# A fused attention and two mixture-of-experts layers: one block more in split products, later weight splits and unread products in gaps

## The chip, the cores and the metric

One core of a Trainium2 chip runs the whole program. The metric is device time in microseconds (us), the median of several executions. TensorE (PE) multiplies, VectorE (DVE), ScalarE (ACT) and GpSimd (POOL) do the rest, SyncE (SP) issues most DMAs. Each engine takes its instructions in the order of its own program and waits on semaphores for the others. A window's clock of 1.00 is TensorE at 2.4 GHz, 0.50 is 1.2 GHz.

## The reference

```python
def _attn_ref(q, k, v):                      # (4, 8, 576, 64)
    q_s = softmax of q over the last axis
    k_s = softmax of k over the sequence
    kv = np.einsum('bhsd,bhse->bhde', k_s, v)
    return np.einsum('bhsd,bhde->bhse', q_s, kv)

def _moe_ref(x, w_gate, w1, w2, capacity):   # x (2304, 512), 8 experts, F = 1024, capacity 576
    logits = x @ w_gate; expert_idx = np.argmax(logits, axis=1)
    # the first 576 tokens of each expert, in order, go through it
    h = np.maximum(np.einsum('ecd,edf->ecf', disp, w1), 0.0)
    y = np.einsum('ecf,efd->ecd', h, w2)
    out[i] = gate_w[i] * y[expert_idx[i], pos[i]]     # 0 for the others

def _moe2_ref(x, w_gate, w1, w2):
    logits = x @ w_gate; order = np.argsort(-logits.flatten())
    for idx in order:                        # greedy: the highest logit first
        tok, e = idx // E, idx % E
        if assigned[tok] >= 0 or counts[e] >= N // E: continue   # 288 tokens each
        assigned[tok] = e; counts[e] += 1
    for e in range(E):
        mask = assigned == e
        out[mask] = np.maximum(x[mask] @ w1[e], 0.0) @ w2[e]
```

## The kernel before

**Attention** comes first; its result goes to memory (`xd`) in rows of tokens, and the first layer's gate logits are formed on the way.

**First layer (`moe1`).** `route1` finds each token's expert and its place, `ilist` makes the list of rows of an expert, `X(t)` transposes 128 gathered rows and splits them into `xh` and `xl`. Products are made in three passes of a split format, hi x hi, lo x hi and hi x lo, each one pass of TensorE (`hidden`, L383 to L385, and L463 to L465). With the data of this run three experts have tokens: `body(0)`, `body(1)` and `last(2)`. `last` also forms the second layer's logits from that expert's rows: `diag` puts the gate weights on diagonals of a free part of `hl` (ACT copies the high parts, L487 subtracts for the low), `turn(g)` transposes a 64-column part of w2 on DVE, copies it on ACT into `w2h` and subtracts on DVE into `w2l` (L491), and `mul(g)` multiplies both parts with the diagonals into `pm`.

**Second layer (`moe2`).** Its tokens are assigned by a search in eight phases, one for each expert. A phase closes an expert and finds its cut among the sorted logits in six steps; a step is a comparison on DVE (`G`), eighteen small products on TensorE (`pc`), a decision on DVE (`sat`, `an`, `ii`), and the next step needs it. `ilist` of a phase then makes the row list (`pp`, `pk`, `pl`, `pz` are its products), and `gather` fetches 3 x 96 rows by indirect DMA into `xg`. This runs between the products of the expert blocks: a planner (`Search`, with model times `Q.pe` and `Q.dv`) adds up what each instruction should take, and puts a search step into the program where its inputs should be there. The order on each engine is thus fixed when the kernel is built.

A block `m` is one expert's 288 tokens: `first(m)` has eight column groups `f` (w1, relu, into `hT` or `hs`), `second(m)` four (`d`: w2, into `yT`). `X(m,d)` transposes the gathered rows, inside `second(m-1)`; `O(m,h)` transposes the results, inside `first(m+1)`, and scatters them. Blocks below `LATE` use plain fp32 products (a pair of TensorE instructions each). Blocks from `LATE` on use the split format: `sp1` and `sp2` make hi (ACT cast) and lo (DVE subtraction) of w1 and w2, into `w1hs`, `w1ls`, `w2hs`, `w2ls`, and the inputs are split as `xhs`, `xls` and `hhs`, `hls`. `sp1(m,k)` stands in `second(m-1)`, `sp2(m,k)` in `first(m)` at even `f`. Before block 0's rows are there, the planner spends `IDLE` us on search steps.

There are two buffers for w1 (`stage`, `w1b`), and one for w2 (`w2b`). `loads` issues a block's w1 when the block two before has no more use for its buffer (`f1`), and w2 when the block before has none (`f2`): at the end of `second(m-1)` for an fp32 block, and after the fourth `sp2` for a split one. `T`, `V` in this layer are wrapped (L770 is the wrapper's line, L777 after the change), so nearly all of the search and the blocks has that one line in the profile, and tiles tell them apart. After `first(4)` the few rows of the last three blocks go through `short` (L1107, L1116, L1128), which this run takes.

Of the kernel before, what the change touches and what calls it, by code (L numbers as in the profile page):

```python
# [324 lines left out]
def moe1(nc,tc,c0,tp,K,W,Q,xd,w1,w2,wg2,yd,L):  # L325

    V=nc.vector; G=nc.gpsimd; T=nc.tensor; A=nc.scalar
    with ExitStack() as ctx:
# [138 lines left out]
        def last(i):  # L467
# [13 lines left out]
            def diag():  # L481

                for r in range(4): A.copy(hl[:,4+r,256:512].rearrange("p (x y) -> p x y",x=2),bc(z1,1,2))
                for a in range(4):
                    p=slice(32*a,32*a+32)
                    d=hl[p,4:8,256:512].rearrange("p r (b a e) -> p r b a e",b=4,a=4)[:,:,:,a]; w=wq[p].rearrange("p (r b) e -> p r b e",r=4)
                    A.copy(d[:,:,:,0:8],w); G.tensor_tensor(d[:,:,:,8:16],w,d[:,:,:,0:8].bitcast(F32),op=ALU.subtract)  # L487
            def turn(g):
                w=wts[g%2]; V.transpose(w,S.w2[:,:,64*g:64*g+64])
                w=w.rearrange("p k (b j) -> p k b j",b=2)  # L490
# [17 lines left out]
            for hf,s in enumerate(ls_):  # L508
                for f in range(8):
                    if hf==0 and f in RS: next(rs,None)  # L510
                    if hf==0:
                        if f>3: mul(f-4)
                    else:
                        if f%2==0: sp2(f//2)
                        if f<4: mul(4+f)
                        if f==3: wlog(); V.tensor_tensor(oj,bc(K.ioj,1,5),bc(liL[:,:,1],2,NJ),op=ALU.is_equal)
                        if f==5:
                            pl=acc.tile([16,256],F32,name="plT",tag="acc"); lmul(pl,0,range(8)); A.copy(lT[0],pl)
                            pl=pst.tile([16,320],F32,name="plT",tag="t")
                        if f==6: lmul(pl,1,range(0,5))  # L520
                        if f==7: lmul(pl,1,(5,))
                    if hf or i: hidden(f,s)
                    if hf==0:
                        if f==1: diag()
                        turn(f)
            def logits():

                V.tensor_tensor(op,bc(K.iop,1,5),bc(liL[:,:,0],2,128),op=ALU.is_equal)
# [31 lines left out]
        def steps(i):  # L560
            if i+1==E:
                with tc.manual_schedule(): last(i)
                return
            with tc.If(n>i+1) as cmp:
                with tc.manual_schedule(): body(i)
                steps(i+1)
            with cmp.Else():
                with tc.manual_schedule(): last(i)
        with tc.manual_schedule():
            nc.sync.dma_start(wgs,wg2.rearrange("(c p) e -> p c e",p=128))  # L570
            for a in range(4): nc.sync.dma_start(wq[32*a:32*a+32],wg2.rearrange("(b i) e -> i b e",i=32))
            route=route1(nc,c0,psl,K,L); nxt=ilist(0)
            next(route)
            next(nxt); next(nxt)
            next(nxt)
            for _ in nxt: pass
            for k in range(4): sp1(k)
            for t in range(2): X(t,True)
            ld(2,0,A)
            for f in range(8):  # L580
                if f in R1: next(route,None)
# [192 lines left out]
class Search:  # L774


    def __init__(self,nc,tc,c,t,K,W,yd,w1,w2):  # L777
        self.nc=nc; self.c=c; self.t=t; self.K=K; self.W=W; self.yd=yd; self.w1=w1; self.w2=w2

        self.w1b=[W.stage.w1,None]; self.w2b=[None,None]  # L780
        self.gens=[]; self.ch=None; self.stop=None; self.blk=-1; self.psum=None; self.xgp=None
        self.pe=self.dv=0.0; self.vo=None
        self.V=Paced(nc.vector,self,self.vcost); self.T=Paced(nc.tensor,self,self.tcost)
        S=self.S=NS()
# [58 lines left out]
    def step(self,x):  # L843
        if x is self.ch and self.stop is not None and self.R[0].sl is not None:
            if self.stop==0:
                self.pe=max(self.pe,x[1]); x[1]=self.pe+0.2; return
            self.stop-=1
        self.pe=max(self.pe,x[1])
        try: r=next(x[0])
        except StopIteration: self.gens.remove(x); return  # L850
        x[1]=self.dv+LATV if r is None else self.dv-0.3 if r=="v" else self.dv+r[0] if type(r) is tuple else self.pe+r
# [4 lines left out]
        self.loads()  # L856
    def idle(self,x):

        for _ in range(int(x*10)): self.pe+=0.1; self.tick()
    def until(self,cond):  # L860

        while not cond():
# [106 lines left out]
    def loads(self):  # L969
# [3 lines left out]
        for b in range(E):  # L973
# [4 lines left out]
            if not B.l1 and (b<2 or self.B[b-2].f1) and (b<BUB or B.xg is not None):  # L978
                B.l1=True
                for k in range(2): nc.sync.dma_start(self.w1b[b%2][:,2*k:2*k+2],self.w1[bass.ds(B.e,1),256*k:256*k+256].rearrange("a (k p) f -> p (a k) f",p=128))  # L980
            if B.l1 and not B.l2 and self.w2b[0] is not None and (b<1 or self.B[b-1].f2):
                B.l2=True
                for k in range(2): nc.sync.dma_start(self.w2b[b%2][:,4*k:4*k+4],self.w2[bass.ds(B.e,1),512*k:512*k+512].rearrange("a (k p) f -> p (a k) f",p=128))


BUB=5
FEW=160
LATE=3


def moe2(nc,tc,t,K,W,Q,yd,w1,w2,out):
    V=Q.V; G=nc.gpsimd; T=Q.T
    with ExitStack() as ctx:
# [50 lines left out]
        def first(m):  # L1044
            r=R[m]; Q.blk=m
            for f in range(8):
                if m>=LATE and f%2==0: sp2(m,f//2)
                if m>0 and f in (1,2,3): O(m-1,f-1)

                if m==E-2 and f>3 and f<7: put(E-1,f-4,zr,False)  # L1050
# [87 lines left out]
        with tc.manual_schedule():  # L1138
            Q.psum=lambda shape,name: psr.tile(shape,F32,name=name,tag="rc")
            Q.xgp=b2  # L1140
            Q.until(lambda: R[0].xg is not None)
            Q.idle(IDLE)
            x0=[pool.tile([128,288],F32,name="pt2",tag=tag) for pool,tag in ((pst,"t"),(pst,"t"),(acc,"acc"),(acc,"acc"))]
# [2 lines left out]
            for u in range(3):  # L1146
                for d in range(4): T.transpose(x0[d][:,96*u:96*u+96],r.xg[:,u,128*d:128*d+128],K.ident[:96,:96])
            for d in range(4): nc.scalar.copy(r.x[:,d],x0[d])
            G.memset(zr,0.0)
            for m in range(BUB-1): first(m); second(m)  # L1150
            first(BUB-1)

# [17 lines left out]
DBG=False  # L1170


LATT=0.64; LATL=1.1; STOP=12; LATD=0.0; LATV=0.0; LATP=0.13; MARG=0.0; TXG=7.87; IDLE=6.63
RS=(1,3,5,7); R1=(1,3,4,6); X1=(2,3,4)


# [53 lines left out]
```

## Time and profile before

| | us |
|---|---|
| median of 3 executions | 613.84 (611.88 to 617.84) |
| profiled execution | 614.9 |
| its span in the trace | 613.2 |
| TensorE busy | 536.0 (87% of the span) |
| DVE busy | 349.6 (57%) |
| ACT, POOL busy | 170.3 (28%), 113.4 (18%) |
| mean granted clock | 0.94 |

The span is what the trace covers; the execution's own time holds 1.7 us more. Busy shares are means over stages with different limits. `x` behind a row is its number of instructions, `<-` in brackets says how long the engine was idle just before and who released it.

### The profile page before, as it was taken

Reading aid. Unit: us, or ns where it says so; the run is one execution under the profiler, and the core shown is the slowest. Engines: PE = TensorE matmul, PEld = TensorE weight load, DVE = VectorE, ACT = ScalarE, POOL = GpSimd, SP = SyncE. Lnnn points to the kernel's source line nnn. Section 1 sums busy time; section 2 is a strip of 40 time slices with the busy share of each in tenths; the row PEclk is TensorE's granted clock in tenths of the full one; section 3 lists DMA queues with packets and bytes.
Section 4 is the critical chain, followed back from the end, with each engine's and each line's share of the span. In section 5 each row is a group of like instructions: output and inputs, shape, how many; then the busy total and the mean of one; then the engine's idle time right before and its main releaser. Section 6 shows DMA issues by size and latency. Waiting matters only on the chain.

```text
span 613.2 us, 10394 instructions
## 1 busy us (share of the span) xinstructions
PE 536.0 (87%) x3995; PEld 450.3 (73%) x3995; DVE 349.6 (57%) x1103; ACT 170.3 (28%) x309; POOL 113.4 (18%) x126
## 2 busy tenths in 40 slices
PE   0699992799999999899995899999999849999993
PEld 0588882689889987898773666667666649999992
DVE  8789879494327331564675657475677747440000
ACT  2244422243323341443000111112023215442120
POOL 4051702203110311200112021030210012250011
PEclk9999997699999999799998698989999969999997
DMA  9982743796304250000044614433243085661401
GB/s 269 310 244 66 246 154 94 231 347 210 139 27 138 78 173 35 14 1 1 18 156 143 217 40 150 149 94 138 59 158 124 14 258 181 228 183 68 166 27 29
DMA packets 54004, 82.43 MB, mean 134 GB/s; under 512 B 11904, under 2 KB 33408, under 8 KB 53936
## 3 DMA queue, kind: packets, MB, share of 16 engines
q1 hardware_dynamic: 38416, 58.82, 29.6%
q0 software_dynamic: 5088, 15.93, 8.5%
q10 hardware_dynamic: 10432, 6.82, 3.7%
q8 instruction: 37, 0.61, 0.4%
q14 instruction: 31, 0.25, 0.1%
HBM read 63.86 MB, written 17.70 MB: 133 GB/s over the span
## 4 chain that ended last, share of the span: by engine, by line
PE 51%; DVE 10%; issue 9%; DMA 3%; ACT 2%; POOL 1%; another core or an unknown queue 0%; POOLq 0%; SPq 0%; ACTq 0%; DVEq 0%
PE pa L770 19%; PE pa L463 3%; PE pa L465 3%; PE pa L464 3%; PE pa L1128 3%; PE pa L1116 3%; PE pa L383 2%; PE pa L384 2%; PE pa L385 2%; PE pa L1107 2%; PE pc L770 2%; DVE G L770 1%; DMA xg<-yd,ib 1%; PE pg L431 1%; DMA w2b<-in_moe_w_dram 1%
## 5 line engine op out<-in xcount | busy, mean ns | idle before, releaser
L383 PE MATMUL pa<-xh,w1h 128*128 128x256 f32 (+1 forms) x192 | 60.1, 313 | 1.0 <-ACT xh L381 0.7
L384 PE MATMUL pa<-xl,w1h 128*128 128x256 f32 (+1 forms) x192 | 58.9, 307 | 0.1
L385 PE MATMUL pa<-xh,w1l 128*128 128x256 f32 (+1 forms) x192 | 58.7, 306 | 0.0
L770 PE MATMUL pa<-h,w2b 128*128 128x288 f32 x192 | 58.1, 433 | 0.0
L968 POOL DMA_INDIRECT xg<-yd,ib x21 | 21.3, 1012 | 122.8 <-issue 53.3
L770 PEld LDWEIGHTS <-G 128*31 128x31 bf16 (+2 forms) x756 | 23.9, 101 | 23.8 <-DVE G L770 13.1
L770 PE MATMUL pa<-x,stage 128*128 128x288 f32 x128 | 40.8, 451 | 0.1
L383 PEld LDWEIGHTS pa<-xh,w1h 128*128 128x128 f32 x192 | 38.3, 199 | 2.7 <-ACT xh L381 1.1
L770 PEld LDWEIGHTS pa<-h,w2b 128*128 128x128 f32 x192 | 34.2, 195 | 7.7 <-issue 0.9
L384 PEld LDWEIGHTS pa<-xl,w1h 128*128 128x128 f32 x192 | 38.3, 199 | 0.5 <-DVE xl L381 0.4
L385 PEld LDWEIGHTS pa<-xh,w1l 128*128 128x128 f32 x192 | 38.4, 200 | 0.0
L1025 POOL DMA_INDIRECT out_dram<-yn,ib x19 | 19.1, 1003 | 103.9 <-ACT yn L1033 52.0
L391 DVE SCALAR_TENSOR_TENSOR hl<-pa,hh 128x256 fp32r<-128x256 f32 (+1 forms) x48 | 21.5, 452 | 29.2 <-ACT hh L390 29.1
L402 POOL DMA_INDIRECT yd<-y,idx x15 | 15.0, 1001 | 112.9 <-ACT y L398 93.4
L770 DVE TENSOR_TENSOR G<-b,th 128x372 bf16<-128x372 f32 (+2 forms) x70 | 33.0, 509 | 1.2
L390 ACT ACTIVATE hh<-pa 128x256 fp32r<-128x256 f32 (+1 forms) x48 | 19.7, 410 | 49.2 <-PE pa L385 46.1
L463 PE MATMUL pa<-w2h,hh 128*128 128x512 f32 (+1 forms) x80 | 33.0, 413 | 0.0
L770 PE MATMUL pc<-g,G 128*31 128x8 bf16 (+2 forms) x756 | 27.8, 170 | 5.3 <-DVE G L770 4.5
L465 PE MATMUL pa<-w2h,hl 128*128 128x512 f32 (+1 forms) x80 | 31.5, 394 | 0.0
L464 PE MATMUL pa<-w2l,hh 128*128 128x512 f32 (+1 forms) x80 | 31.3, 391 | 0.0
L770 PEld LDWEIGHTS pa<-x,stage 128*128 128x128 f32 x128 | 23.6, 203 | 5.7 <-issue 0.4
L1053 ACT ACTIVATE h<-pa 128x288 f32<-128x288 f32 x24 | 9.8, 410 | 62.1 <-PE pa L770 62.1
(380 smaller groups left out, 1259.3 us busy)
## 6 DMA issues: line engine op xcount, KB each, us to landing
stage<-in_moe_w_dram SPq DMA_DIRECT2D x18, 1024.0 KB, 5.4
w2b<-in_moe_w_dram SPq DMA_DIRECT2D x12, 1024.0 KB, 5.9
w1b<-in_moe_w_dram SPq DMA_DIRECT2D x8, 1024.0 KB, 7.2
yd<-z ACTq DMA_DIRECT2D x1, 4608.0 KB, 26.5
km<-in_k_dram SPq DMA_DIRECT2D x4, 1024.0 KB, 10.1
vm<-in_v_dram SPq DMA_DIRECT2D x4, 1024.0 KB, 9.5
xd<-xs SPq DMA_DIRECT2D x8, 512.0 KB, 2.6
qm<-in_q_dram SPq DMA_DIRECT2D x3, 1024.0 KB, 10.4
```

The source lines that it names most:

```text
L383: T.matmul(ps,wh,xh_,start=first,stop=False)
L384: T.matmul(ps,wh,xl_,start=False,stop=False)
L385: T.matmul(ps,wl,xh_,start=False,stop=last)
L390: A.activation(hh[:,f,s],pa,AF.Relu)
L391: V.scalar_tensor_tensor(hl[:,f,s],pa,0.0,hh[:,f,s].bitcast(F32),op0=ALU.max,op1=ALU.subtract)
L463: T.matmul(pa,hh[:,k,ts],W.w2h[:,k],start=(k==0),stop=False)
L464: T.matmul(pa,hh[:,k,ts],W.w2l[:,k],start=False,stop=False)
L465: T.matmul(pa,hl[:,k,ts],W.w2h[:,k],start=False,stop=(k==7))
L770: return f(*a,**k)
L968: nc.gpsimd.indirect_dma_start(out=B.xg[:,h],out_offset=None,in_=self.yd,in_offset=bass.IndirectOffsetOnAxis(ap=B.idx[:,h:h+1],axis=0),bou ...
L1025: s_=G.indirect_dma_start(out=out,out_offset=bass.IndirectOffsetOnAxis(ap=R[m].idx[:,h:h+1],axis=0),in_=src,in_offset=None,bounds_check=N- ...
L1116: for k in range(4): T.matmul(pa,w1_[:,k,128*f:128*f+128],x[:,k,0:FEW],start=k==0,stop=k==3)
```

## The change

- `LATE` is 2: blocks 0 and 1 stay in fp32, blocks 2, 3 and 4 use split products (before: 3 and 4).
- The first split block (`m==LATE`) has its four `sp2` at `f` 4 to 7; later ones at even `f`, as before.
- Block 0's w2 load is issued behind its row copies: a flag `x0`, and a one-element ACT copy from the rows into `w2b` that the load has to wait for. `IDLE` falls from 6.63 to 2.2, so block 0's transposes come earlier in TensorE's program.
- `keep(n)` adds n products of a constant with itself, 128 x 128 in bf16, into a tile `pw` that nobody reads: 24, 36, 72, 10 and 6 in the first layer's opening, and some dozens in the wait for the second layer's first rows.
- In the last expert, the low parts in `diag` are subtracted on DVE instead of GpSimd, and the eight `turn`s are spread otherwise over the column groups: none at `f` 0, one at 1, two at 2, then one each.

```diff
@@ last(i): diag, and the column groups
-                    A.copy(d[:,:,:,0:8],w); G.tensor_tensor(d[:,:,:,8:16],w,d[:,:,:,0:8].bitcast(F32),op=ALU.subtract)
+                    A.copy(d[:,:,:,0:8],w); V.tensor_tensor(d[:,:,:,8:16],w,d[:,:,:,0:8].bitcast(F32),op=ALU.subtract)
...
-                        turn(f)
+                        for g in ((),(0,),(1,2),(3,),(4,),(5,),(6,),(7,))[f]: turn(g)
@@ moe1, opening
+        def keep(n):
+
+            pw=acc.tile([128,128],F32,name="pw",tag="acc")
+            for _ in range(n): T.matmul(pw,K.ones,K.ones,start=True,stop=True)
...
+            keep(24)
             next(route)
+            keep(36)
...
             for _ in nxt: pass
+            keep(72)
             for k in range(4): sp1(k)
-            for t in range(2): X(t,True)
+            X(0,True); keep(10); X(1,True); keep(6)
@@ Search
+        if self.keep and x[1]-self.pe>0.2: self.keep(int((x[1]-self.pe-0.1)*14))
         self.pe=max(self.pe,x[1])
...
-        for _ in range(int(x*10)): self.pe+=0.1; self.tick()
+        for z in range(int(x*10)):
+            if self.keep: self.keep(1+z%2)
+            self.pe+=0.1; self.tick()
...
-            if B.l1 and not B.l2 and self.w2b[0] is not None and (b<1 or self.B[b-1].f2):
+            if B.l1 and not B.l2 and self.w2b[0] is not None and (self.x0 if b<1 else self.B[b-1].f2):
...
-LATE=3
+LATE=2
@@ first(m)
-                if m>=LATE and f%2==0: sp2(m,f//2)
+
+                if m==LATE and f>3: sp2(m,f-4)
+                elif m>LATE and f%2==0: sp2(m,f//2)
@@ moe2, opening
+            pw=[]
+            def keep(n):
+
+                if not pw: pw.append(acc.tile([128,128],F32,name="pw",tag="acc"))
+                for _ in range(n): nc.tensor.matmul(pw[0],K.ones,K.ones,start=True,stop=True)
+            Q.keep=keep
             Q.until(lambda: R[0].xg is not None)
             Q.idle(IDLE)
...
             for d in range(4): nc.scalar.copy(r.x[:,d],x0[d])
+
+            nc.scalar.copy(Q.w2b[0][0:1,0,0:1],r.x[0:1,3,0:1]); Q.x0=True; Q.loads()
             G.memset(zr,0.0)
+            Q.keep=None
...
-IDLE=6.63
+IDLE=2.2
```

DVE before, at the start of block 3's first half, the first split block. `zh` ends an earlier row list, `w2ls` is the first subtraction of block 3's w2, and `scr` to `sb` belong to the search's last row lists; TensorE's `pp` reads `sb`.

```order
L770 TENSOR_TENSOR zh<-z_14162,z_13903 96x1
L770 TENSOR_TENSOR w2ls<-w2b,w2hs 128x1024
L770 SCALAR_TENSOR_TENSOR scr<-closed,r_69 128x8
L770 TENSOR_REDUCE e_966<-scr 128x1
L770 TENSOR_SCALAR ei_976<-e_966 1x1
L770 COPY w__947<-alive 128x18
L770 MEMSET w__947 128x18
L770 SCALAR_TENSOR_TENSOR sb<-rst_128,w__947 128x36
```

DVE after, in block 2's first half, now the first split block, from its third column group to the fifth (`hls` is the low part of one group's result, `G`, `sat`, `ii`, `th` are a search step).

```order
L777 SCALAR_TENSOR_TENSOR hls<-pa,hhs 128x288
L777 TENSOR_TENSOR G<-b,th 128x6x31
L777 TENSOR_TENSOR pre<-pre,ii 128x1
L777 TENSOR_SCALAR sat,an<-pc 31x8
L777 TENSOR_SCALAR ii<-pa_13922 128x1
L777 SCALAR_TENSOR_TENSOR th<-cand_122,ii,pre 128x31
L777 TENSOR_TENSOR G<-b,th 128x12x31
L777 SCALAR_TENSOR_TENSOR hls<-pa,hhs 128x288
L777 TENSOR_TENSOR w2ls<-w2b,w2hs 128x1024
L777 TENSOR_TENSOR G<-b,th 128x6x31
```

The subtraction of w2 has moved from ahead of everything in that half to behind the fourth `hls`, and the search's steps of phase 5 and 6 stand around it.

SP before, its loads from the fifth expert's number (`ei`) on: w2 is block 2's and the two DMAs of `stage` are block 4's w1.

```order
L977 TENSOR_LOAD ei_973
L977 ISA x2
L983 ISA
L983 DMA w2b<-in_moe_w_dram 128x4x512
L983 ISA
L983 DMA w2b<-in_moe_w_dram 128x4x512
L980 ISA
L980 DMA stage<-in_moe_w_dram 128x2x1024
```

SP after, from the same row.

```order
L987 TENSOR_LOAD ei_973
L987 ISA x2
L990 ISA
L990 DMA stage<-in_moe_w_dram 128x2x1024
L990 ISA
L990 DMA stage<-in_moe_w_dram 128x2x1024
L993 ISA
L993 DMA w2b<-in_moe_w_dram 128x4x512
```

Block 4's w1 now stands ahead of block 2's w2; the w2 loads of blocks 3 and 4 follow.

TensorE before, at the second layer's opening: the end of phase 1's last step (`pc`, 32 wide, and its count `pa`), and block 0's row transposes.

```order
L770 LDWEIGHTS G
L770 MATMUL pc<-g,G 32x8
L770 LDWEIGHTS onesb
L770 MATMUL pa_12421<-satb,onesb 128x8
L770 MATMUL pt_12447<-ident,xg_12272 128x96
L770 MATMUL pt_12448<-ident,xg_12272 128x96
```

TensorE after, in the same place.

```order
L777 LDWEIGHTS onesb
L777 MATMUL pa_12519<-an,onesb 128x1
L1157 LDWEIGHTS onesb
L1157 MATMUL pw<-onesb 128x128
L1157 LDWEIGHTS onesb
L1157 MATMUL pw<-onesb 128x128
...
L777 MATMUL pt_12530<-ident,xg_12425 128x96
L777 MATMUL pt_12531<-ident,xg_12425 128x96
```

The transposes stand three search steps earlier, and unread products fill the place ahead of them. In the blocks that follow, the halves (first, second, first, ...) of blocks 0 to 4 hold 6, 5, 6, 5, 6, 2, 0, 0 and 0 steps before, and 5, 6, 6, 4, 5, 1, 5, 1 and 0 after.

## Rows read from the trace of the kernel before

**Rows 1.** Windows, half blocks 0 to 4: start:end, us, each engine's busy us, clock, DMA share, GB/s.

```profile
343.00:368.00 25.00, 24.85 (x182) 16.93 (x182) 15.36 (x64) 3.80 (x11) 3.10 (x3) 0.88 0.29 106
368.00:394.50 26.50, 25.47 (x213) 18.03 (x213) 16.76 (x76) 3.21 (x8) 3.14 (x3) 0.94 0.36 116
394.50:420.40 25.90, 24.70 (x197) 17.07 (x196) 16.80 (x74) 4.91 (x11) 5.96 (x6) 0.93 0.34 115
420.40:445.00 24.60, 23.91 (x213) 17.15 (x213) 16.81 (x76) 3.20 (x8) 3.16 (x3) 1.00 0.39 129
445.00:469.80 24.80, 23.50 (x203) 16.25 (x202) 17.98 (x84) 4.98 (x12) 2.87 (x3) 1.00 0.27 91
469.80:493.40 23.60, 21.37 (x159) 15.09 (x155) 17.06 (x70) 6.97 (x12) 1.08 (x2) 1.00 0.27 91
493.40:519.30 25.90, 17.54 (x135) 16.90 (x135) 15.04 (x55) 8.77 (x15) 5.35 (x5) 0.80 0.77 248
519.30:534.00 14.70, 14.19 (x110) 13.96 (x110) 6.73 (x9) 6.88 (x13) 3.08 (x3) 1.00 0.75 255
534.00:548.00 14.00, 14.00 (x110) 13.99 (x109) 7.74 (x11) 8.68 (x15) 7.14 (x6) 1.00 0.44 145
```

**Rows 2.** Chain of waits ahead of block 3: start, us, what.

```profile
492.08 6.08 DMA w2b<-in_moe_w_dram
...
499.26 1.22 DVE w2ls L770
```

**Rows 3.** Grouped instructions, TensorE, 501 to 548: count, busy, mean ns, idle before.

```profile
L770 PE MATMUL pp<-sb,Ls 128*128 128x1 bf16 x2 | 0.2, 177 | 7.9 <-DVE sb L770 7.9
```

**Rows 4.** TensorE's timeline in block 1 (two rows), and the chain in block 4.

```profile
427.50 4.29 PE L770 MATMUL pa<-h,w2b 128*128 128x288 f32 x17
431.72 0.74 PE L770 MATMUL pc<-g,G 128*63 128x8 bf16 x18
...
539.99 7.99 PE pa L770 x60
```

**Rows 5.** TensorE's timeline behind the wait: first two and last of ten products.

```profile
501.86 0.44 PE L770 MATMUL pa<-xhs,w1ls 128*128 128x288 f32 x1
502.10 0.44 PE L770 MATMUL pa<-xhs,w1hs 128*128 128x288 f32 x1
...
504.31 0.44 PE L770 MATMUL pa<-xhs,w1ls 128*128 128x288 f32 x1
```

**Rows 6.** Timeline, second layer's opening (SP's queue, POOL, TensorE), and the page's DMA list.

```profile
331.41 0.97 SPq L983 DMA_DIRECT2D w2b<-in_moe_w_dram  x2
334.59 0.95 POOL L968 DMA_INDIRECT xg<-yd,ib  x1 [0.30 <-issue]
340.55 2.47 PE L770 MATMUL pt<-ident,xg 96*128 96x96 f32 x12 [1.19 <-DMA xg<-yd,ib]
...
xg<-yd,ib POOLq DMA_INDIRECT x21, 3.4
```

**Rows 7.** Windows at half clock: first layer's opening, last expert, second layer's opening.

```profile
112.84:116.50 3.66, 3.51 (x14) 3.22 (x15) 0.67 (x1) 0.19 (x1) 0.00 (x0) 0.50 0.70 203
253.20:263.40 10.20, 9.30 (x48) 8.75 (x47) 6.54 (x16) 3.99 (x10) 1.89 (x3) 0.50 0.00 0
343.00:348.60 5.60, 5.55 (x15) 3.91 (x15) 3.79 (x14) 1.34 (x5) 0.00 (x0) 0.50 0.89 361
```

**Rows 8.** Timeline, first layer: opening (TensorE), last expert (TensorE, DVE).

```profile
108.77 1.11 PE L379 MATMUL pt<-ident,xg 128*128 128x128 f32 x4 [5.25 <-DMA xg<-xd,idx]
...
255.35 0.47 PE L770 MATMUL pm<-w2h,hl 128*64 128x256 f32 x1 [0.90 <-POOL hl L487]
...
270.66 0.69 DVE L770 TENSOR_TENSOR w2l<-spare,w2h 128x512 fp32r<-128x512 f32 x1 [0.69 <-ACT w2h L491]
```

**Rows 9.** DVE's timeline: one weight subtraction, one subtraction of a result.

```profile
474.37 1.22 DVE L770 TENSOR_TENSOR w1ls<-w1b,w1hs 128x1024 fp32r<-128x1024 f32 x1
...
505.23 0.46 DVE L770 SCALAR_TENSOR_TENSOR hls<-pa,hhs 128x288 fp32r<-128x288 f32 x1
```

More of the change, by code (lines that the diff above doesn't have):

```diff
@@ L780, in __init__ @@
         self.w1b=[W.stage.w1,None]; self.w2b=[None,None]
-        self.gens=[]; self.ch=None; self.stop=None; self.blk=-1; self.psum=None; self.xgp=None
+        self.gens=[]; self.ch=None; self.stop=None; self.blk=-1; self.psum=None; self.xgp=None; self.x0=False; self.keep=None
         self.pe=self.dv=0.0; self.vo=None
@@ L1170 @@
 DBG=False
-LATT=0.64; LATL=1.1; STOP=12; LATD=0.0; LATV=0.0; LATP=0.13; MARG=0.0; TXG=7.87; IDLE=6.63
+LATT=0.64; LATL=1.1; STOP=12; LATD=0.0; LATV=0.0; LATP=0.13; MARG=0.0; TXG=7.87; IDLE=2.2
 RS=(1,3,5,7); R1=(1,3,4,6); X1=(2,3,4)
```

## The prediction, made before the changed kernel ran

> **What bounds the kernel now.** I read the profile in the order in which a stage gives itself away: first the windows over the second expert layer, cut at its half blocks [rows 1], then the chain of waits and the grouped waits of TensorE where one window falls out of line [rows 2, 3], then the timeline for what one product costs [rows 4, 5], then the openings [rows 6, 7] and the last expert of the first layer [rows 7, 8], and last what VectorE pays for a split block [rows 9]. Executions of this kernel shown here differ by about 1% (611.88 to 617.84), so 1%, or 6.1 us, is what a measurement can tell from no change.
>
> Blocks 0 to 4 up to the jump into the short blocks take nine half blocks, 343.0 to 548.0, 205.0 us. TensorE is busy nearly throughout in the first five of them, so there its own instructions set the time. Two things are not work. In 493.4:519.3 it is busy for 17.54 of 25.90 us, at a mean clock of 0.80: block 3's w2 load can start only when block 2 has read the one w2 buffer, the chain goes through the 6.08 us of that load into ACT's cast and DVE's subtraction [rows 2], and the search's small operations stand behind that subtraction in DVE's order, so TensorE waits 7.9 us for `sb` [rows 3]. And in the first three windows the clock is 0.88 to 0.94.
>
> **One block split rather than fp32.** Seventeen fp32 instructions start over 427.50 to 431.72, 0.248 each; a product is two of them, 0.497. Sixty split products take 7.99, 0.133 each [rows 4]. A block has 64 products by the one way and 192 by the other: 31.8 against 25.6, so 6.2 us less.
> The Trainium skill, page "TensorE: Matmul & The Clock Gate", section "Back-to-back issue gap", gives N/2.4 + 2.5 ns for an isolated product, 122.5 ns at 288 columns; by that estimate the split block would take 23.5 and the term be 8.3. The measured row has 133 ns, and the measurement decides.
>
> **The wait at block 3.** The first split block is now block 2, and only it subtracts w2 in its second half, from its fifth column group on. From the end of the block before, four column groups pass, 48 products at 0.133 = 6.4 us, with output transposes and some three search steps (about 1.3 each, below) 11 us, before DVE comes to the subtraction; load and cast need 6.1 and about 1 [rows 2]. That is cover by about 4 us. Blocks 3 and 4 get their w2 load when the block before has split its copy, a whole half block ahead. So the 7.9 us go, and with them the low clock behind the gap: products start 0.24 apart from 501.86 to 504.31 [rows 5], some 13 by 0.107 more than 0.133, 1.4. Together 9.3. What is late next is the search behind DVE, below.
>
> **The half blocks one by one.** From the windows [rows 1]: a split first half takes 14.0 (the ninth window, no search step in it), a split second half 14.7 (the eighth), which is 12.8 of products and 1.2 or 1.9 of transposes. So an fp32 half without search is 15.9 + 1.2 = 17.1, or 17.8. Windows four and five hold five and six search steps: (24.6 - 17.8)/5 = 1.36 and (24.8 - 17.1)/6 = 1.28, so a step costs TensorE 1.3. By the order the nine halves have 6, 5, 6, 5, 6, 2, 0, 0, 0 steps before and 5, 6, 6, 4, 5, 1, 5, 1, 0 after: three of the opening's steps come behind block 0's transposes now, and cost 3.9 in blocks where they cost nothing in the opening's wait. Unknown is what a step costs when DVE also splits weights. A split half adds to DVE four subtractions of 1.22 and, in a first half, eight of 0.46 [rows 9]: 8.6. DVE is busy 16.81 with five steps and 17.98 with six [rows 1], 3.2 a step. Five steps and 8.6 are 24.6 us of DVE, where TensorE needs 14.0 + 6.5 = 20.5: those are the ends for the first halves of blocks 2 and 3, and I take 23, nearer to DVE's because the search goes through both engines in turn. In the second half of block 1, which now splits w1, the ends are 17.8 + 5.2 = 23.0 and 26.2, since the sixth window, with such a split and two steps, stands 3.2 over its 20.4; I take 24.6. The halves after, by the formula with what is added:
> block 0: 25.0 less one step, 23.7, and 17.8 + 7.8 = 25.6 (26.5 before; the dip of its clock, between close steps, has nine or ten products ahead of it now); block 1: 24.9, 24.6; block 2: 23.0, 16.9; block 3: 23.0, 16.7 (14.7 and one step's 1.3, with 0.9 and 0.7 for the split next to it); block 4's first half 15.0, one over its 14.0 for the end of the search. The sum is 193.4, 11.6 less than 205.0. It contains the 6.2 and the 9.3, and about 2 of the dips' clock, against 3.9 of steps and some 2 for DVE.
>
> **The opening.** Before, block 0's w2 load is issued at 331.41, ahead of the last gather (334.59), whose rows reach TensorE at 340.55: 5.96 us, against a median of 3.4 for these gathers [rows 6]. With w2 behind the rows, 2.5 go; the bounds are 0 (w1 of block 1 is still on the queues) and 2.5, and I take 2.5, since the row says what a gather takes without that neighbour. Its reader is second(0), over 20 us later: cover enough. The unread products cost nothing while TensorE waits for rows; whether the clock then is 2.4 GHz is the second case below.
>
> **The first layer.** In 112.84:116.50 the clock is 0.50 with 3.51 us of products [rows 7]; at the full one that is 1.75 less, and I count 1.7 (bounds 0 and 2.2, with the transposes). The 72 products stand in a wait of 5.25 [rows 8]. From 0.24 for 288 columns, 128 take 0.107 at the low clock and all 72 take 7.7, at the full one half of it: the price is 2.4 late in the bad case, nothing in the good one.
> In the last expert, a wait of 0.90 for GpSimd's subtraction goes, since DVE does it [rows 8], and 10.2 us at clock 0.50 hold 9.30 of products [rows 7]. But DVE, by transposes and subtractions in turn, ends its last w2l only at 270.66 + 0.69 [rows 8], with sp2's own right behind; by the changed order this chain is as long. I count 0.5, bounds +3 (the small subtractions now stand ahead of DVE's transposes) and -4. Attention and the short blocks at the end are the same.
>
> **Sum.** 11.6 + 2.5 + 1.7 + 0.5 = 16.3. The profiled execution took 614.9 (span 613.2 and 1.7 around it), 1.1 over the median; 614.9 - 16.3 = 598.6, by the median 597.5. **I predict 598.** With the ends for the search alone (20.5 or 24.6, 23.0 or 26.2) it is 592 to 603.
>
> **Rivals.** *The clock holds.* The unread products keep 2.4 GHz through the opening of the second layer and the turn stage: half of 5.55 and of 9.30 us [rows 7], 2.8 and 4.6, less 0.5 counted: 598 - 7 = 591. For it: those stretches are busy at 0.50. Against it: products stop when rows come, and the last expert gets none of its own.
> *The wait only moves.* Block 2's w2 load stands on SP's queue behind block 4's w1 load; if that, or its sharing of the queues, makes it over 4 us late, DVE stops at the first subtraction as before, with the search behind it. The price lies up to 7.9 + 1.4; I take 8: 606. Against it: block 4's w1 needs only the stage buffer, which is read out while block 1's second half still runs.
> *The search sets the pace in split blocks, and the clock falls.* This is the one that ends slower. A split product covers 0.133 where an fp32 one covers 0.497, so with ten steps in the first halves of blocks 2 and 3 TensorE runs out between steps; behind the gap of before it did, and products started 0.24 apart [rows 5]. At that pace the 384 products of blocks 2 and 3 cost 41 more, 639; half of them 618. It is slower than before from about 150 of them on. Against it: the sixth window had split work on DVE and two steps, and held clock 1.00 [rows 1].
> *The change doesn't do what it says.* The load behind the rows moves nothing, the products run at the low clock and delay the first layer's rows: 2.5 + 1.7 + 2.4 = 6.6 more, 605.
>
> **Chances.** The forecast 0.60 (its own range 591 to 604), the clock holds 0.14, the wait moves 0.13, the search at a low clock 0.06, no effect at the openings 0.07. The second, third and fifth end over 1% faster, too; misjudged terms add up across cases, so I leave 0.09 for within 1% and 0.05 for slower by over 1%, and 0.86 for faster. The range, 588 to 609, takes in the second case and the third, and leaves out the fourth and some of each side.
>
> **What would show it.** Right: no idle time before a `pp` or `sb` in blocks 2 to 4 above 2 us; block 2's products at 0.133; first halves of blocks 2 and 3 between 20.5 and 24.6; the last gather landing in about 3.5 us; clock 1.00 from 113 us on. Wrong: a w2ls in block 2 that waits for its DMA; a granted clock near 0.5 in block 2 or 3; DVE busy over nine tenths of those halves with TensorE waiting for `G` or `sat`; block 0's first product no earlier against the end of the search.

## The result, and the profile after

The changed kernel takes 620.45 us (median of 20, 616.72 to 623.18) against 613.99 before (20 executions): ratio 1.0103, 95% interval 1.0078 to 1.0129. It is slower by 1%, where 598 was forecast. The profiled execution took 623.18, 2.7 over the median, with a span of 621.5 and a mean clock of 0.947. In two of the experiments below, e3_late2 and e6_pool, some executions ran in a slower state; their times and ratios go by the others, but their traces are of a slower one.

The windows over the same half blocks as [rows 1], and behind them block 4's second half, made past the jump to the short blocks, in the columns of [rows 1]:

```profile
340.40:367.70 27.30, 26.19 (x180) 17.68 (x181) 15.53 (x69) 3.93 (x11) 3.11 (x3) 0.81 0.51 177
367.70:394.60 26.90, 25.52 (x212) 18.01 (x212) 17.11 (x78) 3.20 (x8) 3.14 (x3) 0.94 0.33 112
394.60:421.70 27.10, 25.52 (x212) 17.89 (x210) 17.03 (x76) 5.14 (x12) 5.91 (x6) 0.94 0.36 108
421.70:443.10 21.40, 20.82 (x155) 14.81 (x155) 17.43 (x62) 6.71 (x12) 0.00 (x0) 1.00 0.42 155
443.10:469.10 26.00, 22.05 (x223) 19.77 (x222) 16.67 (x58) 8.74 (x15) 5.69 (x6) 0.93 0.53 176
469.10:486.40 17.30, 15.62 (x135) 14.90 (x135) 16.50 (x53) 6.92 (x13) 0.00 (x0) 1.00 0.32 106
486.40:509.90 23.50, 22.41 (x224) 20.03 (x223) 16.88 (x59) 8.68 (x15) 3.20 (x3) 0.93 0.25 75
509.90:532.10 22.20, 18.57 (x158) 17.24 (x156) 16.50 (x66) 6.88 (x12) 0.00 (x0) 0.92 0.13 45
532.10:550.40 18.30, 15.80 (x132) 14.87 (x131) 12.05 (x48) 6.91 (x12) 11.72 (x12) 1.00 0.84 270
550.40:570.40 20.00, 17.88 (x104) 15.83 (x105) 3.71 (x8) 3.25 (x7) 2.28 (x3) 0.83 0.56 208
```

The single hole of [rows 3] is gone: `pp` waits 0.2 us in all. But the nine halves take 210.0, more than the 205.0 of before, and the tenth takes 20.0 (14.7 before, from 547.8 to 562.5). Two fp32 halves of block 0 and 1 still have a clock of 0.94, and block 3's second half (22.2) and block 4's first (18.3) are far above the 14.7 and 14.0 that they took before. In those two, DVE is busy for 16.5 and 12.1 us (6.7 and 7.7 before), with work of the search that before was over by then.

What TensorE waited for between 340 and 572 (us in total, times, longest):

```profile
PE pa L777 <- DVE sat L777: 4.8, 8, 1.9
PE pl L777 <- DVE rh L777: 4.8, 5, 1.2
PE pk L777 <- DVE mksb L777: 4.2, 3, 2.2
```

All three are links of the search. Before, the same three were 0.7, 2.8 and 2.7 between 340 and 550. The timeline of one of the waits for `rh`, in block 1:

```profile
414.71 0.60 PE L777 MATMUL pl<-rh,OH 128*32 128x18 bf16 x18 [1.11 <-DVE rh L777]
415.24 0.88 PE L777 MATMUL pa<-x,w1b 128*128 128x288 f32 x2
416.05 0.18 PE L777 MATMUL pa<-an,onesb 63*128 63x1 bf16 x1
416.16 2.29 PE L777 MATMUL pa<-x,w1b 128*128 128x288 f32 x4
```

A row list's products `pl` stand directly behind a step's 18 small products `pc`, TensorE idles 1.11 us there, and the four fp32 instructions behind take 2.29 where 17 took 4.29 in [rows 4]: the clock has fallen to 1.2 GHz. Such falls begin at 361, 388, 415 and 446, each within 2 us of such a wait.

The end of the search, on DVE's timeline (`zi` is its last number), and the chain of waits at the jump (start, us, what):

```profile
543.10 0.14 DVE L777 CAST zi<-few 1x1 int32<-1x1 f32 x1
```

```profile
544.68 5.17 DMA stage<-in_moe_w_dram
549.85 0.58 issue
550.42 0.63 PE pa L1119 x3
```

Before, `zi` came at 513.0, 35 us ahead of the jump. Now it comes at 543.1; block 6's w1, whose expert number comes just before it, is issued at 544.68, lands at 549.85, and TensorE makes its first product behind the jump at 550.42. It has stood idle for only 0.7 us by then; behind the jump it stops three times more, without a releaser in the profile (us in total, times, longest), and from 552.3 it runs at 1.2 GHz for 6.8 us:

```profile
PE pa L1119 <- issue: 2.1, 3, 1.0
```

### The profile page after: what moved, and what is told of

Its sections match the earlier page's. It is cut to its first block, busy times and chain, and to the rows that moved or that the text cites. A ratio compares the mean times of both kernels' runs of the same rounds, so it can differ in the third digit from the quotient of the medians.

```text
span 621.5 us, 10907 instructions
## 1 busy us (share of the span) xinstructions
PE 550.1 (89%) x4240; PEld 470.8 (76%) x4240; DVE 363.6 (59%) x1127; ACT 177.6 (29%) x318; POOL 109.2 (18%) x122
## 4 chain that ended last, share of the span: by engine, by line
PE 35%; issue 24%; DVE 12%; DMA 2%; POOL 2%; ACT 1%; another core or an unknown queue 1%; POOLq 0%; SPq 0%; ACTq 0%
PE pa L777 14%; PE pa L1140 3%; PE pa L1128 3%; PE pa L1119 3%; PE pc L777 2%; PE pa L463 2%; PE pa L465 1%; PE pa L464 1%; DVE w1ls L777 1%; DVE G L777 1%; PE py L777 1%; POOL yd L402 1%; DMA stage<-in_moe_w_dram 1%; DVE eq L777 1%
## 5 line engine op out<-in xcount | busy, mean ns | idle before, releaser
L777 PE MATMUL pa<-h,w2b 128*128 128x288 f32 x128 | 39.2, 438 | 0.0
L390 ACT ACTIVATE hh<-pa 128x256 fp32r<-128x256 f32 (+1 forms) x48 | 19.7, 410 | 48.2 <-PE pa L385 47.5
L777 PE MATMUL pa<-xhs,w1hs 128*128 128x288 f32 x96 | 30.8, 321 | 0.0
L777 PE MATMUL pa<-xhs,w1ls 128*128 128x288 f32 x96 | 30.5, 317 | 0.0
L777 PE MATMUL pa<-xls,w1hs 128*128 128x288 f32 x96 | 29.9, 312 | 0.0
L777 PEld LDWEIGHTS pa<-h,w2b 128*128 128x128 f32 x128 | 23.3, 198 | 6.4 <-issue 1.5
```

What stands on the lines that cost most here:

```text
L390: A.activation(hh[:,f,s],pa,AF.Relu)
L777: return f(*a,**k)
```

## The experiments

Each ratio is against the kernel before as it ran beside that experiment (medians of 612.9 to 615.6 us), so where two experiments are close, the ratios tell more than the times.

**Only LATE put back (e1_late3).**

```diff
-LATE=2
+LATE=3
```

> The changed kernel with one number put back: LATE is 3, so blocks 0 to 2 are fp32 and block 3 is the first split block, with its w2 subtractions in the second half of its column groups. Theory (the search is late because its steps fall into split blocks, where DVE also splits weights): the search ends in block 3's first half again, the wait for w2 there is gone, and the time falls to about 605 (602 to 608). Rival (what costs is the rest: three steps behind block 0's rows, the unread products): 618 or more, since block 2 is back at 6 us more of products.

615.82 (609.49 to 617.93), ratio 1.0009 [0.9963, 1.0056]. Neither: 4.6 less than the changed kernel, but 11 over the theory's 605. Its blocks 0 and 1 take 107.9, with four falls of the clock in them, and DVE stands still for 4.2 us in block 3. So the rest of the change costs, too.

**Only the rule for w2 (e2_w2half), on the kernel before.**

```diff
-                if m>=LATE and f%2==0: sp2(m,f//2)
+                if m==LATE and f>3: sp2(m,f-4)
+                elif m>LATE and f%2==0: sp2(m,f//2)
```

> The kernel before with only the rule that the first split block subtracts w2 from its fifth column group on (LATE stays 3). Both theories: the 7.9 us wait and the low clock behind it go, 604 to 607. If the wait was cover for work of the search that now comes due instead: 610 to 614.

602.11 (601.58 to 602.33), ratio 0.9826 [0.979, 0.9863]. Its windows over block 2 and block 3's first half:

```profile
441.50:466.90 25.40, 24.09 (x216) 16.75 (x214) 18.20 (x84) 5.37 (x13) 2.87 (x3) 1.00 0.29 96
466.90:489.70 22.80, 20.58 (x144) 14.59 (x141) 17.83 (x76) 6.59 (x12) 0.98 (x1) 1.00 0.23 91
489.70:506.20 16.50, 15.77 (x135) 14.97 (x134) 12.82 (x48) 8.66 (x15) 5.25 (x6) 1.00 0.97 332
```

The half of 25.9 in [rows 1] takes 16.5 at clock 1.00: 9.4 us, the forecast's 9.3. This one rule is worth more than the whole change. e1_late3 is this kernel with the opening's and the first layer's parts of the change: it is 14 slower, and its nine halves take 210.2 where they take 193.8 here.

**Only LATE at 2 (e3_late2), on the kernel before.**

```diff
-LATE=3
+LATE=2
```

> The kernel before with only LATE at 2: block 2 split, its w2 subtracted at even column groups behind its load. Theory (search late in split blocks): slower than before, 618 to 626, with the search's last products in block 4 and block 4's second half waiting. Rival (a split block by itself gives its 6 us): about 608.

610.7 (604.08 to 611.9), ratio 0.9939 [0.9898, 0.998]: between the two. In the trace `zi` comes at 538.3, in block 4's first half, as the theory had it; but that is still 10 us ahead of the jump, and block 4's second half took 14.7, where the theory had it waiting.

**Without the 24 products in attention (e4_no24).**

```diff
-            keep(24)
             next(route)
```

> The changed kernel without the 24 unread products that the order puts between the last products of attention. Theory (they delay the last attention products, for which DVE waits 2.5 us rather than 0.7): 2 us less, about 618.4, and the first layer's opening 2.1 earlier in the trace. Rival (that delay was a variation of the run): 620.5.

620.97, ratio 1.0115 [1.005, 1.0181]: the rival. The first layer's transposes start at 108.9 here and at 111.1 in the changed kernel, but of the other kernels with the 24 products six start them at 108.9 to 109.1, too, and three (e5_open, e9_fill, e11_pl_late3) at 110.4 to 110.9. Whether the products bring the late starts was not settled; no kernel without them starts later than 109.6.

**The second layer's opening as before (e5_open), on the changed kernel.**

```diff
-(self.x0 if b<1 else self.B[b-1].f2)
+(b<1 or self.B[b-1].f2)
...
-            Q.keep=keep
...
-            nc.scalar.copy(Q.w2b[0][0:1,0,0:1],r.x[0:1,3,0:1]); Q.x0=True; Q.loads()
...
-IDLE=2.2
+IDLE=6.63
```

> The changed kernel with the second layer's opening as before: block 0's w2 load ahead of its rows, 6.63 us of search steps in the wait, no unread products there. Theory (three steps moved behind block 0's rows cost more in blocks 0 and 1 than the earlier rows bring, by about 3): 615 to 618, with blocks 0 and 1 shorter by about 5 and starting about 4 later. Rival (the opening's part gains what was forecast): 623.

605.01, ratio 0.9803 [0.9754, 0.9852]: 15 less, where the theory gave 2 to 5. Block 0 starts 4.8 later, blocks 0 and 1 take the same, and the gain is further on. Its windows over blocks 2 and 3 and block 4's first half:

```profile
447.60:465.20 17.60, 17.60 (x172) 16.19 (x171) 13.09 (x51) 8.38 (x14) 2.92 (x3) 1.00 0.44 133
465.20:485.00 19.80, 17.84 (x151) 16.93 (x150) 15.85 (x45) 6.88 (x12) 0.00 (x0) 0.91 0.32 106
485.00:505.00 20.00, 19.80 (x206) 17.82 (x205) 15.46 (x50) 8.68 (x15) 3.24 (x3) 1.00 0.29 87
505.00:523.80 18.80, 16.14 (x142) 15.08 (x141) 16.59 (x72) 6.88 (x12) 1.00 (x1) 1.00 0.17 55
523.80:539.20 15.40, 15.17 (x130) 14.73 (x129) 12.14 (x39) 8.69 (x15) 9.71 (x9) 1.00 0.91 307
```

They sum to 91.6, against 107.3 in the changed kernel: with three steps fewer in the blocks, `zi` comes at 532.55, 6.6 ahead of the jump, and block 4's second half takes 14.7 again. Beside e2_w2half, where block 2 is fp32, this also shows what a split block brings: block 2 takes 37.4 rather than 48.2, and block 3 with block 4's first half 54.2 rather than 45.2. Of 10.8 gained, 9.0 are given back.

**Low parts on GpSimd (e6_pool), on the changed kernel.**

```diff
-            (V if Q.gens or k%2 else G).tensor_tensor(lo,
+            G.tensor_tensor(lo,
```

> The changed kernel with every low part of a weight split subtracted on GpSimd rather than on DVE. By the order the search then ends in block 3, not in block 4. Theory (DVE holds both the search and the weight splits in blocks 2 to 4, so the search ends late and the jump to the short blocks waits): blocks 2 to 4 fall from 127 us to about 112, time 603 to 609. Rival (the search is late for its own chain of steps, not for DVE's other work): 617 to 621. If GpSimd is too slow for the weights, TensorE waits for w1ls or w2ls from GpSimd: 620 or more.

630.0 (626.07 and 634.0), ratio 1.023 [1.0145, 1.0315]: the third outcome by its time, so it says nothing on the first two. In the trace (an execution of 636.91) TensorE waits for GpSimd's low parts only once, 1.2 us, and longest for DVE (8.5 us for `xls`), so by which way GpSimd delays the blocks was not told. A group of its instructions on POOL (count, busy, mean ns, idle before):

```profile
L1018 POOL TENSOR_TENSOR w2ls<-w2b,w2hs 128x1024 fp32r<-128x1024 f32 x12 | 28.4, 2378 | 29.8 <-ACT w2hs L1017 27.2 <-PE pa L777 2.6
```

2.38 us each, twice DVE's 1.22 [rows 9]; block 2's second half takes 30.5.

**Row lists' products later (e7_plgap on the changed kernel, e8_half_pl on e2_w2half).** The same edit in both:

```diff
-        yield (0.4,)
+        yield (1.9,)
         pl=self.psum([32,9,3],"pl2")
```

> The changed kernel in which the planner places the row list's products (pl) 1.5 us later, so that block products stand where TensorE waited 1.1 us for rh right behind a step's 18 products. Theory (the falls of the clock in blocks 0 to 2 follow that wait, each worth about 2 us): no stretch at 1.2 GHz between block 0's opening and block 2, 611 to 615. Rival (they come from elsewhere): same falls, 618 to 621.

> The kernel before with the w2 rule alone (602.1 measured) and the row list's products placed 1.5 us later. Theory: the one fall of the clock left in blocks 0 to 2 goes, 598 to 601. Rival: 602.

e7_plgap 600.66 (598.58 to 603.97), ratio 0.9771 [0.973, 0.9812]: 20 less than the changed kernel, more than the theory gave. e8_half_pl 602.22, ratio 0.9767 [0.9732, 0.9803]: by the time the rival; its ratio is 0.6% under e2_w2half's, with overlapping intervals, so the two are not told apart. The fall in block 0 did go (blocks 0 and 1 take 95.7 for 100.3), but another came at 455, in block 2 (first half 27.3 for 25.4). In e7_plgap, block 0's second half, block 1's first and block 3's second:

```profile
360.30:384.30 24.00, 23.51 (x212) 16.63 (x210) 16.92 (x74) 3.61 (x9) 1.48 (x3) 1.00 0.39 131
384.30:408.20 23.90, 23.41 (x196) 16.34 (x195) 16.38 (x74) 4.59 (x10) 5.46 (x6) 1.00 0.37 121
...
495.70:513.50 17.80, 16.30 (x156) 15.42 (x155) 13.70 (x50) 6.98 (x12) 0.00 (x0) 1.00 0.15 55
```

The clock holds, and `zi` comes 9.4 earlier against block 0's start than in the changed kernel. One fall is left, at 412 to 419, in block 1's second half, behind a wait of 1.1 us for another link, `sat`. Blocks 0 and 1, and then blocks 2 to 4 up to the jump:

```profile
335.51:434.80 99.29, 96.10 (x757) 66.54 (x758) 67.43 (x284) 18.99 (x42) 11.93 (x12) 0.94 0.41 142
434.80:531.08 96.28, 89.07 (x863) 81.85 (x862) 79.95 (x282) 39.99 (x69) 16.80 (x17) 1.00 0.39 130
```

Together 195.6, against 210.0 in the changed kernel and the 193.4 of the forecast: the same split blocks cost little more than forecast once these products stand later.

**Unread products in that wait (e9_fill), on the changed kernel.**

```diff
+        pw=self.psum([128,192],"pl2"); pl=pw[0:32,0:27].rearrange("p (a b) -> p a b",b=3)
+        for _ in range(16): self.nc.tensor.matmul(pw[:,64:192],K.ones,K.ones,start=True,stop=True)
```

> The changed kernel with 16 unread 128 x 128 bf16 products ahead of each row list's products (pl), written to an unread part of pl's own PSUM tile; everything else keeps its order. They fill the 1.1 us in which TensorE waited for rh. Theory (the wait and the fall of the clock behind it cost the time, not the order of the steps): no stretch at 1.2 GHz between block 0's opening and block 2, 602 to 609. Rival (placing pl later gained by shifting the search's steps): 617 to 621.

610.06 (607.31 to 610.69), ratio 0.9942 [0.9914, 0.997]: 10 less, just above the theory's 602 to 609. Its blocks 0 and 1:

```profile
340.40:438.30 97.90, 96.64 (x804) 68.31 (x805) 67.04 (x284) 19.10 (x42) 12.18 (x12) 0.97 0.43 144
```

They take 97.9 rather than 102.7, with no fall of the clock behind block 0's opening until 517, and block 4's second half takes 14.7. So the waits with their falls are worth about half of e7_plgap's gain. The other half lies in blocks 2 to 4 (96.3 in e7_plgap, 104.5 here); there e7_plgap has the steps in another order, which was not tried by itself.

**Three parts undone on e7_plgap.** e10_pl_open has the opening's edit of e5_open, e11_pl_late3 LATE at 3, e12_pl_first the first layer as before (no `keep`, `diag` on GpSimd, `turn(f)` at each f).

> The kernel with the row lists' products placed later (600.7 measured), with the second layer's opening as before: block 0's w2 load ahead of its rows, the full search in the wait, no unread products there. If the opening's part brings its forecast 2.5 once the waits are filled: 603. If the three steps behind the rows cost as much as the earlier rows bring: 599 to 601. If they still push the search's end into the jump: under 598.

611.31, ratio 0.9962 [0.9928, 0.9995]: none of the three. Against e7_plgap, the way from the last expert's second product to block 0 is 5.1 longer, and `zi` comes 5.4 ahead of the jump, with this window behind it:

```profile
538.60:559.10 20.50, 17.62 (x106) 15.78 (x105) 3.44 (x7) 2.36 (x6) 3.81 (x4) 0.83 0.62 228
```

That is 5.8 over 14.7, as in the changed kernel. The earlier rows are worth about 5 by themselves, twice the 2.5 of the forecast, and the three steps cost 1.0 in the nine halves here (194.6 for 195.6).

> The kernel with the row lists' products placed later (600.7 measured), with LATE at 3: block 2 in fp32 again. By the forecast's terms block 2 split is worth 6.2 less what the search costs in split halves (about 2 to 4): 603 to 605. If a split block costs the search more than it gains: 596 to 600.

606.01, ratio 0.9897 [0.9841, 0.9954]: 5 over e7_plgap (8 by the ratios), near the forecast's terms; but in the traces, 7.5 apart, 4.3 lie ahead of block 0, and the ten halves take 213.5 against 210.3. With the waits filled, splitting block 2 brings 3 or less, since e11_pl_late3 also has a stop of DVE of 3.2 in block 2 (last section).

> The kernel with the row lists' products placed later (600.7 measured), with the first layer as before: no unread products there, diag's low parts on GpSimd, one turn in each column group. By the forecast's terms 2.2 us slower, 603; if the clock in the first layer's opening and in the last expert is worth its whole half, 605 to 607; if nothing, 600.7.

612.73, ratio 0.9987 [0.9958, 1.0016]: outside all three, and inconclusive. In the trace (an execution of 608.68) block 0 starts only 1.6 later than in e7_plgap; the rest is in block 2's and block 4's first halves (27.1 and 22.3 for 22.0 and 17.6), whose program is the same in both.

**An eighth of the low parts (e13_eighth), on the changed kernel.** It leaves out the low part of seven eighths of the second layer's split weights, which GpSimd sets to zero once.

```diff
-            (V if Q.gens or k%2 else G).tensor_tensor(lo,src[:,sl],hi.bitcast(F32),op=ALU.subtract)
+            (V if Q.gens or k%2 else G).tensor_tensor(lo[:,:,0:128],src[:,sl][:,:,0:128],hi[:,:,0:128].bitcast(F32),op=ALU.subtract)
...
+            for z in (1,3): G.memset(sw[z].rearrange("p k f -> p (k f)").bitcast(F32),0.0)
```

> The changed kernel in which the second layer's weight splits subtract only an eighth of the columns for the low part (the rest of it is zero, so part of the products' precision is left out): 16 DVE subtractions of 1.22 us in blocks 2 and 3 become about 0.2. Theory (DVE carries the search and the splits, and each split block's subtractions lengthen the search's chain): the search ends some 15 us earlier than in the changed kernel, TensorE waits nowhere at the jump, 602 to 608. Rival (only the waits ahead of pl and the three moved steps make the search late): at most 4 us, 616 to 620.

602.2 (600.43 to 603.36), ratio 0.9809 [0.9778, 0.984]: the theory, with the waits ahead of `pl` left as they are (4.4 us). The end of its search, and block 3's second half and block 4's first:

```profile
515.47 0.14 DVE L777 CAST zi<-few 1x1 int32<-1x1 f32 x1
```

```profile
504.10:520.70 16.60, 15.30 (x131) 14.81 (x132) 10.16 (x56) 6.62 (x12) 5.85 (x6) 1.00 0.82 279
520.70:534.90 14.20, 14.20 (x111) 14.19 (x110) 4.91 (x11) 8.68 (x15) 5.56 (x6) 1.00 0.81 255
```

Counted from block 0's start, the search ends after 176.8 rather than 202.7 us. The sixteen subtractions of blocks 2 and 3, shorter by 1 us each, are 16 of the 26; what the rest is made of was not told apart (block 4's splits, and steps that the planner places sooner).

**Block 6's w1 behind the jump (e14_jump), on the changed kernel.** `loads` leaves that load out, and `short` begins with it (the flag that tells `loads` is not shown):

```diff
...
+            for k in range(2): nc.sync.dma_start(Q.w1b[(BUB+1)%2][:,2*k:2*k+2],w1[bass.ds(R[BUB+1].e,1),256*k:256*k+256].rearrange("a (k p) f -> p (a k) f",p=128))
             for h in range(3): put(E-1,h,zr)
...
```

> The changed kernel with block 6's w1 load issued behind the jump to the short blocks, not ahead of it. Theory (block 4's second half took 20.0 rather than 14.7 because that load, which starts when the search ends, has to land before TensorE passes the jump): 14.7 there, 614 to 617. Rival (the jump waits for the search's last number itself): 20 there, 619 to 622.

607.49, ratio 0.9895 [0.9872, 0.9918]. Block 4's second half:

```profile
541.90:556.60 14.70, 14.70 (x106) 13.78 (x106) 1.76 (x5) 1.61 (x4) 4.12 (x5) 1.00 0.90 315
```

It is 5.3 less, as the theory had it. But that the load has to land before TensorE passes the jump is not borne out. In e7_plgap it is issued 1.2 us ahead of TensorE's first product behind the jump (531.08), its two DMAs take 5.8 us or more, and the half still takes its 14.7 (SP's queue, the loads' times, block 4's second half):

```profile
529.90 0.95 SPq L990 DMA_DIRECT2D stage<-in_moe_w_dram  x2
DMA to landing us min/median/max: 5.8/8.5/11.1
531.08:545.80 14.72, 14.72 (x106) 13.80 (x105) 1.76 (x5) 1.61 (x4) 6.05 (x7) 1.00 1.01 363
```

Nor is it how far ahead the load is issued. At 5.7, 5.7 and 4.0 us ahead of that product the half takes 20.0, 20.3 and 20.5 (the changed kernel, e4_no24, e10_pl_open); at 5.5, 4.4 and 2.7 it takes 14.7 (e5_open, e9_fill, e12_pl_first). So in three kernels of seven that issue it within 6 us of the jump something is lost, in TensorE's stops behind the jump and the clock; why in these three stays open.

The gain is 13: 3.1 more lie ahead of block 0 and 2.8 in block 2's first half, where DVE did not stand still (last section). The program there is the same; still all four executions are over 7 us under the fastest of the changed kernel's twenty, and what brings that was not found.

**Unread products on e2_w2half (e15_half_fill).** e9_fill's edit.

> The kernel before with the w2 rule alone (602.1 measured) and the 16 unread products ahead of each row list's products. Theory (each fall of the clock behind the wait for rh costs about 2 us; one is left there): 599 to 601. Rival: 602, or 603 if the products delay the row lists.

607.63 (603.5 to 610.48), ratio 0.9884 [0.9828, 0.994]: 5 slower than e2_w2half (4 by the ratios), a miss. 3.3 of it lie ahead of block 0, where the programs are the same but for one row list; block 2's first half has a new fall of the clock (27.7 for 25.4). Filling one wait does not always pay.

By the ratios the fastest are e8_half_pl (0.9767) and e7_plgap (0.9771); e5_open (0.9803) and e2_w2half (0.9826), too, are some 2% under the kernel before. e13_eighth (0.9809) leaves a part of the precision out.

## Why the prediction was wrong, step by step

- **The wait at block 3: right.** 9.3 forecast, 9.4 in e2_w2half; in the changed kernel, `w2ls` of block 2 waits for no load.
- **The split block: right in itself, wrong in the price of the search beside it. This is the step that failed.** The nine halves took 210.0 for 193.4. The forecast put DVE's double load into the first halves of blocks 2 and 3 alone (23.0 each; 26.0 and 23.5 measured) and gave block 3's second half and block 4's first 16.7 and 15.0; they took 22.2 and 18.3. DVE was busy for only 16.7 and 16.9 us in those first halves, not for the 24.6 that I summed: the engine was far from full. The search is one chain through DVE, whose links stand behind the split work in DVE's order, and that lengthens it (e13_eighth): it does not stay in the halves in which its steps were counted, but ends later, here by 32.8 us against block 0's start. e5_open beside e2_w2half is the same thing without the opening: 10.8 gained, 9.0 given back. The time of blocks 2 to 4 was 107.3 for 94.6, 12.7 of the miss; some 3 of it is DVE's stop in block 2 (23.2 for 26.0 in e14_jump). These blocks take 91.9 with an eighth of the low parts (e13_eighth), 91.6 with the three steps ahead of block 0 (e5_open) and 96.3 with `pl` later (e7_plgap). And e1_late3, with block 2 in fp32, loses as much elsewhere: 7.6 in blocks 0 and 1 and 8.4 in block 3's first half, beside e2_w2half. So the price comes from the split work, the moved steps and the place of `pl` together; the share of one of them alone was not measured.
- **"The short blocks at the end are the same": false.** I did not ask what a later end of the search holds up. 5.3 of the miss lie in block 4's second half, and are gone in e14_jump. What costs them stays open: a late end is not enough, since `zi` comes 6.6, 6.1, 3.8 and 2.2 us ahead of the jump in e5_open, e9_fill, e12_pl_first and e7_plgap at no loss, and 7.3 ahead in the changed kernel.
- **"The dip of its clock ... has nine or ten products ahead of it now": false.** The products stand ahead of `pc`; the wait is behind it, at `pl`, and has no product in it. Three falls in blocks 0 and 1 where two were (a fourth is in block 2): they took 102.7 for 98.8. e9_fill removed the falls and 10 us, 4.8 of them in blocks 0 and 1.
- **The opening: right in direction, 2.5 forecast, 4.4 measured** between the last expert's second product and block 0; e10_pl_open has 5.1. But its three steps were priced at 3.9, and in the changed kernel, with the opening's gain against them, cost 15 net (e5_open); with `pl` later, 1.0 in the nine halves (e10_pl_open). The unread products did not hold the clock there, against the rival "The clock holds": it is 1.2 GHz from 334 to 347, 7.1 us of it in block 0's first half, against 5.6 before.
- **The first layer: 2.2 forecast, nothing measurable.** Its hidden products took 32.7 us for 32.5, since the clock fell at 115 to 118, right behind the unread products; in e7_plgap, where it fell at 98 to 101, they took 31.2. The last expert has 3.4 us at 1.2 GHz rather than 10.2, and took 42.5 for 42.8. That the chain of turns paces it, as forecast, is half of it: with no fall of the clock it takes 39.8 in e2_w2half, whose program there is that of before, and 41.0 in e7_plgap, where it is the changed one. By these single traces the clock was worth 3.0 there, and the new order costs 1.2 of them (before, e2_w2half, e7_plgap):

```profile
244.90:287.70 42.80, 40.91 (x281) 38.73 (x282) 25.01 (x52) 18.48 (x41) 3.65 (x7) 0.88 0.02 6
245.10:284.90 39.80, 37.01 (x280) 34.89 (x281) 24.63 (x52) 18.02 (x41) 3.67 (x7) 1.00 0.03 6
243.00:284.00 41.00, 37.06 (x280) 34.89 (x281) 25.84 (x56) 18.22 (x41) 1.34 (x3) 1.00 0.02 6
```

The third rival, the search setting the pace in split blocks, was the mechanism as far as the runs show one; its place was right and its chance of 0.06 far too low. It was priced by products at a low clock; falls in blocks 2 to 4 (at 446, 491 and 525, some 10 us at 1.2 GHz, so at most 5 lost) were the smaller share.

## What to carry to other kernels

When work is moved beside a chain that runs through the same engine, do not only sum that engine's busy time: count what the work puts between the chain's links, along the whole chain, and follow its end to whoever needs the last result; the price is not only in the stage where the work is put. A wait is covered by what stands between it and the instruction ahead of it, so read the order at the waiting instruction itself. And try the parts one by one: here one rule of two lines had most of the gain.

## What the runs showed of the hardware

**The clock is worth more than its waits.** Behind waits of 1.1 us among small products stand stretches of some 3.5 us at 1.2 GHz. Not each such wait has one: in e2_w2half the wait of 1.03 for `rh` at 376.0 has, the wait of 1.20 at 403.8 has not. From 336 to 572, the changed kernel has 38.8 us at 1.2 GHz, the kernel before 29.8, e2_w2half 13.4. TensorE is busy for 36.1 of the 38.8, and half of that at most is lost: up to 18 us, 3% of the span. The Trainium skill, page "TensorE: Matmul & The Clock Gate", section "What's actually happening", says of the slow start of a kernel's products that "the ramp penalty is <1% of a typical kernel span"; this case's falls come anew inside the span, and that figure is no measure for them.

**An engine that stands still without a releaser.** In the changed kernel, on DVE's timeline:

```profile
454.02 0.16 DVE L777 TENSOR_SCALAR_CACHE_REDUCE sat<-pc 63x8 f32<-63x8 f32 x1 [3.45 <-remote]
```

The product it needs had ended at 451.9, so 2.1 us of the 3.45 have no reason in the profile. Stops like it (2.7 to 4.2 us, once in a run) are in the changed kernel, e1_late3, e4_no24, e10_pl_open (on ACT), e11_pl_late3 and e12_pl_first, each beside or within 2 us of a row of four to eight indirect DMAs that POOL issues back to back. The kernel before has at most three in a row, and no stop; but e7_plgap and seven others (e3_late2, e5_open, e6_pool, e8_half_pl, e9_fill, e13_eighth, e14_jump) have rows of four to eight, too, and no stop. Whether the rows cause it was not tried and stays open. Such a stop is one of the things by which kernels with the same program in a stretch differ there, by up to 5 us.
